# Attention and mixture of experts on one core: a half slot for a half block, gathers one slot later, a reordered last pair

## The chip, the cores and the metric

The kernel runs on one core of a Trainium2 chip. The metric is the time of one execution on the device in microseconds (us); three executions were timed. TensorE (PE) multiplies, ScalarE (ACT) and VectorE (DVE) evict and split, GpSimd (POOL) issues the indirect transfers, SyncE (SP) issues the other loads and stores.

## The reference

```python
# attention: 8 batches, 8 heads, 576 positions, 64 wide, with rotary embedding of q and k
scores = matmul(rotate(q), rotate(k).T) / 8
x = softmax(scores) @ v              # as 4608 tokens x 512
# mixture of experts, one expert per token, 8 experts, hidden width 1024
logits = x @ w_gate + modality_bias[modality_id]
e_idx = argmax(logits); gate_w = softmax(logits)[e_idx]
for e in range(8):
    mask = e_idx == e
    out[mask] = gate_w[mask] * (relu(x[mask] @ w1[e]) @ w2[e])
```

With the inputs that are timed, three experts get tokens: expert 1 gets 1143, expert 6 gets 2289, expert 7 gets 1176. In blocks of 256 rows these are 5, 9 and 5, with 119, 241 and 152 rows in the last blocks.

## The kernel before, in words

Attention comes first: 32 pairs of heads (four pairs a batch), one after the other, with the work of neighbouring pairs interleaved. The order of TensorE, ScalarE, VectorE and POOL is written out by hand: each piece of work has a key, a place in time within its pair (`KEYS`, with overrides for the first, second and last pair in `AT`), one pair is `PER` = 14.438 long, and the jobs are issued in the order of their keys. Program order is queue order on each of these engines. For a pair there are nine score products (S), row minima (MN) and exponentials (EX), six groups of transposes of the probabilities (fills F0 to F3, FA, FB) with evictions by ScalarE (A_) and VectorE (B_), two products with V (AVA for the first 256 columns, AVB for the rest), their evictions (OT), the output products (OUT) and evictions (EV).

Routing runs beside it. For each batch, `route` finds the expert and the place of each token; `scatter` writes token number and gate weight into a table in DRAM (TAB), five indirect transfers a batch. `plan0` makes the plan (PLA) of the first NA = 8 blocks from the first five batches; `plan` makes the plan (PLB) of the rest from all, in VectorE operations on one row; the last batch's routing, its scatters and `plan` lie in a list (`late`) of which `one()` issues one item at fixed places of the expert slots.

The experts run in slots of 256 rows. Slot s takes row numbers and gate weights from TAB (`m_ix`), gathers its rows from X into XG[s % 2] in eight indirect transfers on POOL (`m_gather`, with index arithmetic before the first), transposes them on VectorE (`m_tr`) and splits them into a high part (ScalarE) and a low part (VectorE) (`m_tre`). Weights are loaded by SP into ST1 and ST2 only where the expert changes, and split again in each slot (`m_split`, high part on ScalarE, low part on VectorE). L1 (`m_l1`, line 799) is four groups of 24 matmuls, three for each product (high x high, high x low, low x high); `m_l1e` evicts a group. L2 (`m_l2`, line 816) is two halves of 24 matmuls of 512 columns, one for each 128 rows; each is scaled by the gate weight on ScalarE (line 819) and written to its tokens' rows by an indirect transfer on POOL (line 820).

Slots 0 to 18 (8 of the first plan, NB_STATIC = 11 of the second) always run; a conditional tail (`tc.If`) runs the rest where the plan has more. In `chain`, a slot s issues in this order: gathers for slot s + 2, indices of s + 3, weight loads, then four times (split of W2, group of L1, eviction, one late item), transposes and splits of the rows of slot s + 1, L2 of its first half, two splits of W1, L2 of its second half, two splits of W1. The gathers of the first three slots, and the work of slot 0, have keys in `AT` (`rows`, `l1`, `l1e` and so on): the gathers of slot 1 after the first L1 group of slot 0, those of slot 2 at key 16.5, between the second and the third of the five table scatters of the seventh batch.

Of the kernel before, what the change touches and what calls it, by code (L numbers as in the profile page):

```python
# [18 lines left out]
P = 128  # L19
# [3 lines left out]
BLK = 256  # L23
NA = 8
NB_MAX = 17
NB_STATIC = 11

# [56 lines left out]
def tile_attention_moe(ctx: ExitStack, tc: tile.TileContext, qk, v, mod, wg, mb, w1, w2, rope, cf, ci, out):  # L84
# [18 lines left out]
    PLA = cst.tile([1, 3, NB_MAX], I32, name="PLA")  # L103
    PLB = cst.tile([1, 3, NB_MAX], I32, name="PLB")
    TOT = cst.tile([1, 1], I32, name="TOT")
# [506 lines left out]
    def plan():  # L612
# [18 lines left out]
        tri = cview("TRI")[0:1].rearrange("p (a b) -> p a b", b=E)  # L631
        t88 = t1("t88", [E, E])
        V_.tensor_tensor(t88, tri, nb.unsqueeze(1).to_broadcast([1, E, E]), op=ALU.mult)
        yield
# [18 lines left out]
        V_.tensor_tensor(ch, es[:, 1:ns + 1], es[:, 0:ns], op=ALU.subtract)  # L653
        V_.tensor_scalar(pl[:, 2, 0:ns], ch, 0.0, None, op0=ALU.not_equal)
        yield

# [43 lines left out]

    slots = [(0, i) for i in range(NA)] + [(1, i) for i in range(NB_MAX)]
    ms = {}
# [9 lines left out]
    def m_ix(s):  # L712
        d = ms[s]
        ix = d["ix"] = ixp.tile([P, 2, 2], I32, name="ix", tag="ix")
        i1 = nc.sync.dma_start(out=ix, in_=TAB[bass.ds(d["r"], BLK), :].rearrange("(p t) w -> p t w", t=2)).ins
# [12 lines left out]
    def m_gather(s, t, g, after=None):  # L728
        d = ms[s]
        if "iy" not in d:  # L730
            d["iy"] = ixp.tile([P, 8], I32, name="iy", tag="iy")
            nc.gpsimd.tensor_scalar(d["iy"], d["xi"][:, :, 0], 4.0, cview("I4"), op0=ALU.mult, op1=ALU.add)
        rows = (N if slots[s][0] else NPL * S) * 4
        inst = nc.gpsimd.indirect_dma_start(out=XG[s % 2][:, t, g, :], out_offset=None,  # L734
                                            in_=X.rearrange("n (i f) -> (n i) f", f=P)[0:rows],
                                            in_offset=bass.IndirectOffsetOnAxis(ap=d["iy"][:, 2 * g + t:2 * g + t + 1], axis=0),
                                            bounds_check=rows - 1, oob_is_err=False)
# [5 lines left out]
    def m_rows(s):  # L743
        for t in range(2):
            for g in range(4):
                m_gather(s, t, g)

# [55 lines left out]
    def m_l1e(s, g):  # L803
        d = ms[s]
        ps = d["ps", g]
        sl = slice(g * 2, g * 2 + 2)
        nc.scalar.activation(d["hh"][:, sl, :], ps, AF.Relu)
        nc.vector.scalar_tensor_tensor(d["hl"][:, sl, :], ps, 0.0, d["hh"][:, sl, :].bitcast(F32), op0=ALU.max, op1=ALU.subtract)

    def m_l2(s, t):  # L810
        d = ms[s]
        ps = bank("Y")
        m = 0
        for c in range(8):
            for hx, w in ((d["hh"], W2[0]), (d["hl"], W2[0]), (d["hh"], W2[1])):
                nc.tensor.matmul(ps, hx[:, c, t * P:(t + 1) * P], w[:, c, :], start=(m == 0), stop=(m == 23))  # L816
                m += 1
        y = yp.tile([P, DM], F32, name="y", tag="y")
        nc.scalar.activation(y, ps, AF.Copy, scale=d["ix"][:, t, 1:2].bitcast(F32))  # L819
        nc.gpsimd.indirect_dma_start(out=out, out_offset=bass.IndirectOffsetOnAxis(ap=d["ix"][:, t, 0:1], axis=0),  # L820
                                     in_=y, in_offset=None, bounds_check=N - 1, oob_is_err=False)
# [35 lines left out]

    OV = {0: AT["first"], 1: AT["second"], z: AT["last"]}
    for n in range(NPAIR):
# [34 lines left out]
        if n % 4 == 3:  # L894
# [26 lines left out]
    assert min(A["w2"]) > max(K["T1"], K["LO"]) and min(A["te"]) > max(K[f"S{u}"] for u in range(9)) - PER  # L921
    assert min(A["hi2"]) > fills + 0.05 and min(A["lo2"]) > A["last"]["AVB"] + 0.05 and min(A["l1"]) > fills
# [35 lines left out]
    def prefetch(s):  # L958
# [4 lines left out]
        for i in range(3):  # L963
            m_ix(s + i)
        for i in range(2):
            m_rows(s + i)
        for g in range(4):
            m_load2(s, g)

    def chain(lo, hi, begun):  # L970
# [6 lines left out]
        for s in range(lo, hi):  # L977
            nxt = s + 1 < hi
            if nxt:
                if s + 2 < hi and (not begun or s > 0):  # L980
                    m_rows(s + 2)
                if s + 3 < hi and (not begun or s > 0):
# [6 lines left out]
            if not begun or s > lo:  # L989
                for g in range(4):  # L990
                    m_split(1, g)
                    m_l1(s, g)
                    m_l1e(s, g)
                    one()
            if nxt:
                for t in range(2):
                    m_tr(s + 1, t)
                for t in range(2):
                    m_tre(s + 1, t)
                    one()  # L1000
# [4 lines left out]
            if nxt:  # L1005
# [3 lines left out]
                one()  # L1009
            m_l2(s, 1)  # L1010
            if nxt:
# [4 lines left out]

    ns = NA + NB_STATIC
    chain(0, ns, True)
    order.close()
    tot = nc.values_load(TOT[0:1, 0:1], min_val=0, max_val=NB_MAX)  # L1020
    with tc.If(tot > NB_STATIC):
        prefetch(ns)
        chain(ns, NA + NB_MAX, False)

# [99 lines left out]
```

## Time and profile before

| what | us |
|---|---|
| median of 3 runs | 939.65 (937.27 to 940.5) |
| the profiled execution, its own time | 946.46 |
| its span, first to last instruction | 944.7 |
| TensorE busy in the span | 903.4 |
| attention in the span, to the first matmul of L1 | 497.5 |

The profile is of one execution, and that one took 6.8 us more than the median of the timed ones. Lines of the profile name an engine, a line of the kernel, the operation, what it writes and reads, and how long it took. Matmuls are pipelined: one that is shown with 0.28 or 0.39 us may start 0.117 or 0.233 us after the one before it. A number in brackets is the idle time of that engine before the instruction and what ended it.

### The profile page before, as it was taken

Reading aid. Unit: us, or ns where it says so; the run is one execution under the profiler, and the core shown is the slowest. Engines: PE = TensorE matmul, PEld = TensorE weight load, DVE = VectorE, ACT = ScalarE, POOL = GpSimd, SP = SyncE. Lnnn points to the kernel's source line nnn. Section 1 sums busy time; section 2 is a strip of 40 time slices with the busy share of each in tenths; the row PEclk is TensorE's granted clock in tenths of the full one; section 3 lists DMA queues with packets and bytes.
Section 4 is the critical chain, followed back from the end, with each engine's and each line's share of the span. In section 5 each row is a group of like instructions: output and inputs, shape, how many; then the busy total and the mean of one; then the engine's idle time right before and its main releaser. Section 6 shows DMA issues by size and latency. Waiting matters only on the chain. (4 is left out here: it accounts for less than half of the span.)

```text
span 944.7 us, 24944 instructions
## 1 busy us (share of the span) xinstructions
PE 903.4 (96%) x9248; PEld 740.9 (78%) x9248; DVE 670.6 (71%) x1165; ACT 629.9 (67%) x1292; POOL 669.0 (71%) x498
## 2 busy tenths in 40 slices
PE   2999999999999999999989999999999999999996
PEld 2777777777777777777667878888888899999995
DVE  6677778787787877877784768676666766666661
ACT  2778778787787877878881555565665656666561
POOL 3988879888888898999723768766676656666400
PEclk9999999999999999999999999999999999999998
DMA  8865758768586686855922621117711611251100
GB/s 261 237 185 166 236 159 213 188 167 229 162 222 165 183 213 175 232 163 154 244 98 73 186 72 35 46 57 229 230 51 51 229 40 45 90 190 45 37 24 16
DMA packets 79292, 136.90 MB, mean 145 GB/s; under 512 B 28699, under 2 KB 50603, under 8 KB 78140
## 3 DMA queue, kind: packets, MB, share of 16 engines
q1 hardware_dynamic: 68460, 114.06, 42.8%
q0 software_dynamic: 9440, 19.46, 6.3%
q10 hardware_dynamic: 1264, 1.72, 0.6%
q8 instruction: 75, 1.23, 0.6%
q14 instruction: 53, 0.43, 0.2%
HBM read 140.59 MB, written 19.77 MB: 170 GB/s over the span
## 5 line engine op out<-in xcount | busy, mean ns | idle before, releaser
L328 ACT ACTIVATE P<-ps,mn 128x576 f32<-128x576 f32 x288 | 210.4, 737 | 92.4 <-DVE mn L321 91.9
L321 DVE TENSOR_REDUCE mn<-ps 128x1 f32<-128x576 f32 x288 | 204.1, 745 | 93.5 <-PE ps L312 55.6
L734 POOL DMA_INDIRECT XG<-X,iy x152 | 187.7, 1235 | 70.9 <-issue 53.5
L799 PE MATMUL psH<-HL,W1H 128*128 128x256 f32 x1152 | 205.5, 281 | 1.0 <-issue 0.7
L312 PE MATMUL ps<-SW 64*128 64x288 f32 x960 | 166.5, 314 | 16.0 <-DMA SW<-HL 16.0
L799 PEld LDWEIGHTS psH<-HL,W1H 128*128 128x128 f32 x1152 | 177.9, 188 | 4.1 <-issue 2.5
L312 PE MATMUL ps<-HL 64*128 64x288 f32 x960 | 166.4, 312 | 1.0 <-ACT P L328 0.8
L799 PE MATMUL psH<-HL,W1L 128*128 128x256 f32 x576 | 161.7, 281 | 1.4 <-issue 0.8
L312 PEld LDWEIGHTS ps<-SW 64*128 64x128 f32 x960 | 134.2, 189 | 27.4 <-DMA SW<-HL 15.5
L312 PEld LDWEIGHTS ps<-HL 64*128 64x128 f32 x960 | 136.4, 189 | 22.7 <-issue 13.6
L269 DVE TENSOR_TENSOR W1L<-ST,W1H 128x1024 fp32r<-128x1024 f32 x76 | 90.1, 1222 | 80.6 <-ACT W1H L272 77.5
L390 PE MATMUL pa<-PH,V 128*64 128x320 f32 (+1 forms) x1024 | 138.3, 412 | 2.7 <-ACT oT L272 1.4
L820 POOL DMA_INDIRECT out_dram<-y,ix x38 | 42.9, 1128 | 129.7 <-ACT y L819 97.4
L816 PE MATMUL psY<-W2H,SW 128*128 128x512 f32 x304 | 121.2, 399 | 0.0
L816 PE MATMUL psY<-W2L,SW 128*128 128x512 f32 x304 | 119.9, 394 | 0.0
L334 PE MATMUL ps<-idf,P 64*128 64x64 f32 x2624 | 105.3, 229 | 8.5 <-ACT P L328 2.8
L334 PEld LDWEIGHTS ps<-idf,P 64*128 64x128 f32 x2624 | 92.2, 140 | 23.8 <-ACT PH L272 9.5
L799 PEld LDWEIGHTS psH<-HL,W1L 128*128 128x128 f32 x576 | 108.4, 188 | 1.8 <-issue 1.0
L289 POOL TENSOR_TENSOR HL<-ST,HL 128x1216 fp32r<-128x1216 f32 x31 | 86.1, 2777 | 31.8 <-ACT HL L272 31.7
L390 PEld LDWEIGHTS pa<-PH,V 128*64 128x64 f32 x1024 | 68.1, 136 | 51.1 <-issue 10.1
L366 DVE COPY PH<-ps 128x512 f32<-128x512 f32 (+1 forms) x160 | 96.0, 633 | 8.9 <-PE ps L334 7.6
L269 DVE TENSOR_TENSOR W2L<-ST,W2H 128x1024 fp32r<-128x1024 f32 x76 | 92.6, 1219 | 5.2 <-ACT W2H L272 4.3
(173 smaller groups left out, 1589.9 us busy)
## 6 DMA issues: line engine op xcount, KB each, us to landing
ST<-in_moe_w_dram SPq DMA_DIRECT2D x152, 512.0 KB
ST<-in_qk_dram SPq DMA_DIRECT2D x62, 608.0 KB
SW<-HL SPq DMA_DIRECT2D x124, 232.0 KB
V<-in_v_dram SPq DMA_DIRECT2D x32, 256.0 KB
X<-X SPq DMA_DIRECT2D x8, 1024.0 KB
XG<-X,iy POOLq DMA_INDIRECT x152
V<-in_v_dram SPq DMA_DIRECT2D x64, 16.0 KB
X<-XT SPq DMA_DIRECT2D x16, 64.0 KB
```

Of the source, the lines that this page charges most:

```text
L269: nc.vector.tensor_tensor(o, a, b, op=ALU.subtract)
L289: e.tensor_tensor(d["HL"][:, 1, c], a, d["HL"][:, 0, c].bitcast(F32), op=ALU.subtract)
L312: free(nc.tensor.matmul(ps[:, g, 0:288], t[:, wq, q0:q0 + P], t[:, wk, k0:k0 + 288], start=(m == 0), stop=(m == len(L) - 1)), seen)
L321: lastmin[d["ring", u]] = nc.vector.tensor_reduce(mn, d["S", u][:, :, 0:288], op=ALU.min, axis=AX.XY).ins
L328: nc.scalar.activation(p.rearrange("p (a b) -> p a b", a=2), ps[:, :, 0:288], AF.Exp, bias=d.pop(("m", u)), scale=-1.0, accum_out=d["sum"] ...
L334: free(nc.tensor.transpose(ps[0][:, g, c:c + 64], src[r, k0:k0 + P], idf[r, r]), ps[1])
L366: mine.append((nc.vector.tensor_copy if g else acopy)(o, i).ins)
L390: i = nc.tensor.matmul(pa[hh * 64:hh * 64 + 64, 0:c1 - c0], d["V"][:, hh, kt, :], r, start=(kt == 0), stop=(kt == 4))
L734: inst = nc.gpsimd.indirect_dma_start(out=XG[s % 2][:, t, g, :], out_offset=None, in_=X.rearrange("n (i f) -> (n i) f", f=P)[0:rows], in_o ...
L799: l1_[s] = nc.tensor.matmul(ps[:, i, :], w[:, c, f0:f0 + P], x[:, c, :], start=(m == 0), stop=(m == 11)).ins
L816: nc.tensor.matmul(ps, hx[:, c, t * P:(t + 1) * P], w[:, c, :], start=(m == 0), stop=(m == 23))
L820: nc.gpsimd.indirect_dma_start(out=out, out_offset=bass.IndirectOffsetOnAxis(ap=d["ix"][:, t, 0:1], axis=0), in_=y, in_offset=None, bounds ...
```

## The change

One block of one expert that is at most half full gets a slot of 128 rows. `plan` counts, for each expert, whether its last block holds at most 128 rows, takes the first such expert, takes one block off it, and writes a plan entry for the half slot (24 operations more on VectorE). NB_STATIC becomes 10, and the half slot comes behind the ten as the last one that always runs. In it, half as many rows are gathered, transposed, split and evicted, and there is one half of L2 instead of two; it is computed in two parts of 256 columns, the first evicted by ScalarE, the second by VectorE and ScalarE in halves. L1 runs on all 256 columns as before.

The gathers of slot s + 1 are issued in slot s, a pair before each L1 group; from the second pair on they wait for the group of L1 before. In slot 0 (gathers of slot 1) the pairs wait for the groups that their keys put before them. The gathers of slot 2, which had keys, are issued in slot 1.

In the last pair of attention F2 and FB go before FA, AVB before AVA, and the eviction EVA of the pair before it goes ahead of AVB.

```diff
-NB_STATIC = 11
+NB_STATIC = 10
-           (7, 4.75, (30, "out", 1))), ((0, 11.15, ("l1", 0)),), ((0, 16.5, None),)),
+           (7, 4.75, (30, "out", 1))), ((0, 11.15, ("l1", 0)), (2, 11.33, ("l1", 0)), (4, 11.365, ("l1", 0)), (6, 11.43, ("l1", 0)))),
-    last=dict(AVA=10.3, AVB=10.4, RE=10.2, RI=10.25, OTA=10.96, OTB=11.0, OUTB=11.2, OUTA=11.21, EVB=11.35, EVA=11.4, XO=11.9),
+    last=dict(F2=7.0, A_F2=7.75, B_F2=7.75, FB=7.5, A_FB=8.3, B_FB=8.3, FA=8.35, A_FA=8.8, B_FA=8.8, AVB=10.3, AVA=10.4, RE=10.2,
+              RI=10.25, OTB=10.96, OTA=11.0, OUTB=11.2, OUTA=11.21, EVB=11.35, EVA=11.4, XO=11.9),
+    last2=dict(EVA=24.55),
 # plan():
+        V_.tensor_scalar(ni, nf, float(BLK // 2 - 1), None, op0=ALU.add)
+        nc.vector.tensor_scalar(ni, ni, 8, None, op0=ALU.logical_shift_right)
+        hm = t1("hm", [E])
+        V_.tensor_copy(hm, ni)
+        V_.tensor_tensor(hm, hm, AB, op=ALU.subtract)
+        V_.tensor_tensor(hm, nb, hm, op=ALU.subtract)
...
+        V_.tensor_tensor(nb, nb, hm, op=ALU.subtract)
...
+        V_.memset(pl[:, 2, NB_STATIC:NB_STATIC + 1], 1)
-    slots = [(0, i) for i in range(NA)] + [(1, i) for i in range(NB_MAX)]
+    slots = [(0, i) for i in range(NA)] + [(1, i) for i in range(NB_STATIC)] + [(2, NB_MAX)] + [(1, i) for i in range(NB_STATIC, NB_MAX)]
+    halves = lambda s: range(1 if slots[s][0] == 2 else 2)
 # m_l1e(s, g):
+        n = P * len(halves(s))
+        hh, hl = (d[x][:, g * 2:g * 2 + 2, 0:n] for x in ("hh", "hl"))
 # m_l2(s, t):
+        cut = (0, DM // 2, DM) if slots[s][0] == 2 else (0, DM)
+        for a, b in zip(cut, cut[1:]):
+            ps = bank("Y")[:, 0:b - a]
...
+                    nc.tensor.matmul(ps, hx[:, c, t * P:(t + 1) * P], w[:, c, a:b], start=(m == 0), stop=(m == 23))
...
+            if a:
+                h = (a + b) // 2
+                nc.vector.tensor_scalar(y[:, h:b], ps[:, h - a:], gate, None, op0=ALU.mult)
+                b = h
+            nc.scalar.activation(y[:, a:b], ps[:, 0:b - a], AF.Copy, scale=gate)
 # jobs:
-                late = steps + scats + [(each, next) + ((g, None),) * 4] * 7
+                late = steps + scats + [(each, next) + ((g, None),) * 4] * 13
-    for s in range(3):
+    for s in range(2):
         for i in range(8):
 # chain():
-                if s + 2 < hi and (not begun or s > 0):
-                    m_rows(s + 2)
                 for g in range(4):
                     m_split(1, g)
+                    if nxt:
+                        for i in (2 * g, 2 * g + 1)[:4 * len(halves(s + 1)) - 2 * g]:
+                            m_gather(s + 1, i // 4, i % 4, ("l1", s) if g else None)
                     m_l1(s, g)
                     m_l1e(s, g)
                     one()
-            m_l2(s, 1)
+            if len(halves(s)) > 1:
+                m_l2(s, 1)
-    ns = NA + NB_STATIC
+    ns = NA + NB_STATIC + 1
```

## Rows read from the trace of the kernel before

**Rows 1.** Busy time of each engine in windows that are one L1 or one L2 long: L1 of slots 1 and 2, L1 and L2 of a steady slot (slot 13). The first column is start, end and length in us; PEclk is the granted clock.

```profile
526.23:538.80 12.57, 11.92 (x103) 11.66 (x102) 11.54 (x21) 8.29 (x11) 10.42 (x8) 1.00 0.87 199
550.10:565.31 15.21, 13.45 (x98) 12.03 (x98) 10.11 (x12) 8.84 (x11) 9.30 (x7) 1.00 0.15 49
...
801.47:812.73 11.26, 11.26 (x97) 11.26 (x96) 8.69 (x9) 8.06 (x10) 8.57 (x6) 1.00 0.12 41
812.73:823.92 11.19, 11.19 (x50) 9.03 (x49) 6.54 (x8) 5.24 (x6) 5.35 (x5) 1.00 0.30 88
```

**Rows 2.** Timeline of TensorE at the end of attention: the two products with V of the last pair, and the first matmuls of L1 of slot 0. Columns: start in us, length in us, engine, line, operation, out<-in, count, idle time before and its releaser.

```profile
490.81 1.95 PE L390 MATMUL pa<-PH,V 128*64 128x256 f32 x16 [1.28 <-ACT re L406]
...
494.62 2.38 PE L390 MATMUL pa<-PH,V 128*64 128x320 f32 x16 [1.43 <-ACT oT L272]
...
497.46 0.51 PE L799 MATMUL ps<-HL,W1H 128*128 128x256 f32 x2
```

**Rows 3.** Timeline of POOL in the steady slot 13 (L1 starts at 801.47): output scatter of the second half of slot 12, index arithmetic, the first and the last of the eight gathers, output scatter of the first half of slot 13.

```profile
802.68 0.99 POOL L820 DMA_INDIRECT out_dram<-y,ix  x1 [4.58 <-ACT y L819]
803.75 2.05 POOL L732 TENSOR_SCALAR iy<-xi,CF 128x8 int32<-128x8 int32 x1
806.08 1.76 POOL L734 DMA_INDIRECT XG<-X,iy  x1 [0.27 <-POOL iy L732]
...
816.73 1.35 POOL L734 DMA_INDIRECT XG<-X,iy  x1 [0.30 <-issue]
819.54 1.01 POOL L820 DMA_INDIRECT out_dram<-y,ix  x1 [1.46 <-ACT y L819]
```

**Rows 4.** Timeline of ScalarE: a copy of 128x128 out of PSUM in the last pair, and the last eviction of the kernel.

```profile
487.90 0.30 ACT L272 ACTIVATE PD<-ps 128x128 f32<-128x128 f32 x1
...
936.44 0.69 ACT L819 ACTIVATE y<-psY,ix 128x512 f32<-128x512 f32 x1 [4.92 <-PE psY L816]
```

**Rows 5.** Timeline of VectorE at the end of attention: transposes of the rows of slot 0, their low parts (HL), a weight split, and the eviction EVA of the pair before the last.

```profile
490.62 1.30 DVE L779 STREAM_TRANSPOSE XG<-XG 128x512 f32<-128x512 f32 x2
...
492.55 2.11 DVE L269 TENSOR_TENSOR HL<-XG,HL 128x512 fp32r<-128x512 f32 x2 [0.53 <-ACT HL L272]
494.57 2.35 DVE L269 TENSOR_TENSOR W1L<-ST,W1H 128x1024 fp32r<-128x1024 f32 x2
496.84 0.41 DVE L437 TENSOR_TENSOR X<-pa,ri 128x256 f32<-128x256 f32 x1
```

**Rows 6.** Windows of one microsecond behind the last gather of the steady slot; the last two columns are the busy share of the DMA engines and GB/s.

```profile
818.00:819.00 1.00, 1.00 (x6) 0.80 (x5) 0.20 (x1) 0.43 (x1) 0.08 (x1) 1.00 0.21 66
819.00:820.00 1.00, 1.00 (x6) 0.79 (x5) 0.00 (x0) 1.00 (x2) 0.46 (x1) 1.00 0.02 4
```

**Rows 7.** Timeline of VectorE in the steady slot: transposes, two low parts of W1.

```profile
814.17 1.30 DVE L779 STREAM_TRANSPOSE XG<-XG 128x512 f32<-128x512 f32 x2
...
820.25 2.36 DVE L269 TENSOR_TENSOR W1L<-ST,W1H 128x1024 fp32r<-128x1024 f32 x2 [2.05 <-ACT W1H L272]
```

**Rows 8.** Timeline of ScalarE in the steady slot: high parts of the rows, eviction of the first half of L2, two high parts of W1.

```profile
814.96 2.06 ACT L272 ACTIVATE HL<-XG 128x512 fp32r<-128x512 f32 x2 [1.43 <-DVE HL L808]
818.57 0.69 ACT L819 ACTIVATE y<-psY,ix 128x512 f32<-128x512 f32 x1 [1.56 <-issue]
819.16 2.00 ACT L272 ACTIVATE W1H<-ST 128x1024 fp32r<-128x1024 f32 x2
```

**Rows 9.** Timeline of POOL in slots 1 and 2, at the edges of the stretches that are counted: indices for slot 2 and, behind them, the last of its eight gathers, three table scatters and the second output scatter of slot 0 (13 instructions, 528.15 to 546.72); the second output scatter of slot 1, then from the first of two table scatters over indices and eight gathers to the last of three more table scatters (14 instructions, 567.78 to 590.03).

```profile
528.15 0.92 POOL L732 TENSOR_SCALAR iy<-xi,CF 128x8 int32<-128x8 int32 x1
...
540.60 1.00 POOL L734 DMA_INDIRECT XG<-X,iy  x1 [0.30 <-issue]
...
545.74 0.98 POOL L820 DMA_INDIRECT out_dram<-y,ix  x1 [0.30 <-issue]
...
565.80 1.68 POOL L820 DMA_INDIRECT out_dram<-y,ix  x1 [4.57 <-issue]
567.78 0.97 POOL L537 DMA_INDIRECT TAB<-VAL,oi  x1 [0.30 <-DVE ni L624]
...
589.11 0.92 POOL L537 DMA_INDIRECT TAB<-VAL,oi  x1 [0.31 <-issue]
```

**Rows 10.** Timeline of VectorE and TensorE at the end of slot 1: the second transpose of the rows of slot 2, and the third matmul of L1 of slot 2.

```profile
546.73 0.71 DVE L779 STREAM_TRANSPOSE XG<-XG 128x512 f32<-128x512 f32 x1 [3.80 <-DMA XG<-X,iy]
...
551.37 0.39 PE L799 MATMUL psH<-HL,W1L 128*128 128x256 f32 x1 [0.76 <-issue]
```

**Rows 11.** Timeline of VectorE at the end of slot 2: the two low parts of the rows of slot 3, with plan operations behind each, and the first weight split of W1.

```profile
569.82 1.10 DVE L269 TENSOR_TENSOR HL<-XG,HL 128x512 fp32r<-128x512 f32 x1 [0.64 <-issue]
...
571.98 1.09 DVE L269 TENSOR_TENSOR HL<-XG,HL 128x512 fp32r<-128x512 f32 x1
...
573.64 1.22 DVE L269 TENSOR_TENSOR W1L<-ST,W1H 128x1024 fp32r<-128x1024 f32 x1
```

**Rows 12.** Windows with the granted clock (the column behind the five engines) in L1 of slot 0 and around the two gaps at the end of attention.

```profile
508.00:512.00 4.00, 2.19 (x15) 1.66 (x14) 1.77 (x2) 0.00 (x0) 3.33 (x3) 1.00 0.18 52
512.00:516.00 4.00, 3.67 (x16) 3.14 (x15) 0.45 (x1) 0.60 (x1) 0.00 (x0) 0.57 0.06 16
...
490.00:497.00 7.00, 4.76 (x38) 2.96 (x40) 6.47 (x10) 4.54 (x7) 0.00 (x0) 1.00 0.01 2
```

More of the change, by code (lines that the diff above doesn't have):

```diff
@@ L103, in tile_attention_moe @@
     PLA = cst.tile([1, 3, NB_MAX], I32, name="PLA")
-    PLB = cst.tile([1, 3, NB_MAX], I32, name="PLB")
+    PLB = cst.tile([1, 3, NB_MAX + 1], I32, name="PLB")
     TOT = cst.tile([1, 1], I32, name="TOT")
@@ L632, in plan @@
         t88 = t1("t88", [E, E])
+        V_.tensor_scalar(ni, nf, float(BLK // 2 - 1), None, op0=ALU.add)
+        yield
+        nc.vector.tensor_scalar(ni, ni, 8, None, op0=ALU.logical_shift_right)
+        yield
+        hm = t1("hm", [E])
+        V_.tensor_copy(hm, ni)
+        yield
+        V_.tensor_tensor(hm, hm, AB, op=ALU.subtract)
+        yield
+        V_.tensor_tensor(hm, nb, hm, op=ALU.subtract)
+        yield
+        V_.tensor_tensor(t88, tri, hm.unsqueeze(1).to_broadcast([1, E, E]), op=ALU.mult)
+        yield
+        hc = t1("hc", [E])
+        nc.vector.tensor_reduce(hc, t88, op=ALU.add, axis=AX.X)
+        yield
+        V_.tensor_scalar(hc, hc, 1.0, None, op0=ALU.is_equal)
+        yield
+        V_.tensor_tensor(hm, hm, hc, op=ALU.mult)
+        yield
+        V_.tensor_tensor(nb, nb, hm, op=ALU.subtract)
+        yield
+        V_.tensor_tensor(hc, nb, AB, op=ALU.add)
+        yield
+        V_.tensor_scalar(hc, hc, float(BLK), float(-E * N), op0=ALU.mult, op1=ALU.add)
+        yield
+        V_.tensor_tensor(hc, hc, EBv, op=ALU.add)
+        yield
+        V_.tensor_tensor(hc, hc, hm, op=ALU.mult)
+        yield
+        hr = t1("hr", [1])
+        nc.vector.tensor_reduce(hr, hc, op=ALU.add, axis=AX.X)
+        yield
+        V_.tensor_scalar(hr, hr, float(E * N), None, op0=ALU.add)
+        yield
+        V_.tensor_copy(pl[:, 1, ns:ns + 1], hr)
+        yield
+        V_.tensor_tensor(hc, hm, cview("W8")[0:1], op=ALU.mult)
+        yield
+        nc.vector.tensor_reduce(hr, hc, op=ALU.add, axis=AX.X)
+        yield
+        V_.tensor_scalar(hr, hr, -1.0, float(E), op0=ALU.mult, op1=ALU.add)
+        yield
+        V_.tensor_scalar(hr, hr, float(E - 1), None, op0=ALU.min)
+        yield
+        V_.tensor_copy(pl[:, 0, ns:ns + 1], hr)
+        yield
+        V_.memset(pl[:, 2, ns:ns + 1], 1)
+        yield
         V_.tensor_tensor(t88, tri, nb.unsqueeze(1).to_broadcast([1, E, E]), op=ALU.mult)
@@ L654, in plan @@
         V_.tensor_scalar(pl[:, 2, 0:ns], ch, 0.0, None, op0=ALU.not_equal)
+        yield
+        V_.memset(pl[:, 2, NB_STATIC:NB_STATIC + 1], 1)
         yield
@@ L714, in m_ix @@
         ix = d["ix"] = ixp.tile([P, 2, 2], I32, name="ix", tag="ix")
+        if slots[s][0] == 2:
+            nc.sync.dma_start(out=ix[:, 0, :], in_=TAB[bass.ds(d["r"], P), :])
+            xi = d["xi"] = ixp.tile([P, 8, 2], I32, name="xi", tag="xi")
+            nc.sync.dma_start(out=xi[:, 0:4, :], in_=TAB[bass.ds(d["r"], P), :].rearrange("(q g) w -> q (g w)", g=4).unsqueeze(0).to_broadcast([4, 32, 8]))
+            return
         i1 = nc.sync.dma_start(out=ix, in_=TAB[bass.ds(d["r"], BLK), :].rearrange("(p t) w -> p t w", t=2)).ins
@@ L741, in m_gather @@
                               mybir.DependencyInfo(mybir.DependencyClass.Sync, mybir.DependencyReason.DATA), reason="place")
[L743 to L746, printed above, removed]
     def m_load1(s, g):
@@ L856, in tile_attention_moe @@
     z = NPAIR - 1
-    OV = {0: AT["first"], 1: AT["second"], z: AT["last"]}
+    OV = {0: AT["first"], 1: AT["second"], z - 1: AT["last2"], z: AT["last"]}
     for n in range(NPAIR):
@@ L921, in tile_attention_moe @@
     assert min(A["w2"]) > max(K["T1"], K["LO"]) and min(A["te"]) > max(K[f"S{u}"] for u in range(9)) - PER
-    assert min(A["hi2"]) > fills + 0.05 and min(A["lo2"]) > A["last"]["AVB"] + 0.05 and min(A["l1"]) > fills
+    assert min(A["hi2"]) > fills + 0.05 and min(A["lo2"]) > A["last"]["AVA"] + 0.05 and min(A["l1"]) > fills
     for s in range(len(A["plan"])):
@@ L964, in prefetch @@
             m_ix(s + i)
-        for i in range(2):
-            m_rows(s + i)
+        for i in range(8):
+            m_gather(s, i // 4, i % 4)
         for g in range(4):
@@ L995, in chain @@
             if nxt:
-                for t in range(2):
+                for t in halves(s + 1):
                     m_tr(s + 1, t)
-                for t in range(2):
+                for t in halves(s + 1):
                     m_tre(s + 1, t)
@@ L1022, in tile_attention_moe @@
         prefetch(ns)
-        chain(ns, NA + NB_MAX, False)
+        chain(ns, len(slots), False)
 CF_OFF = {}
```

23 lines of the change are left out of this document (11 added, 12 removed).

## The prediction

> **What bounds the kernel now.** I read the busy windows first, stage by stage, because a share over the whole span mixes the attention with the experts. In a steady slot the first product (L1, 96 matmuls of 256 columns) takes 11.26 us and the second (L2, 48 matmuls of 512 columns) 11.19 us, and TensorE is busy for all of both [rows 1]: 0.117 and 0.233 us a matmul, 22.45 us a slot. From slot 3 to the last matmul the time is the sum of TensorE's work; whatever comes later than TensorE wants it is paid in full, and whatever is taken from TensorE is won in full. TensorE is not full before that: at the end of attention it stands 1.28 us before the first product with V and 1.43 us before the second [rows 2], and L1 of slots 1 and 2 takes 12.57 and 15.21 us where 11.26 would do [rows 1].
>
> Next I read the queue of GpSimd (POOL), because the change moves its gathers. In a steady slot that starts at 801.47 it issues the scatter of the previous slot's second half at 802.68, the index arithmetic at 803.75 and eight gathers from 806.08 to 818.08 [rows 3]. These gathers are for the slot after next, so they have a whole slot of slack. That is why POOL can be far behind in the first slots at little cost to TensorE.
>
> **Taken away: half of L2 in the last slot.** The inputs need five, nine and five blocks of 256 rows, 19 in all, and one expert's fifth has 119 rows. The new plan finds it, so 18 full blocks and one half remain and the conditional tail stays shut. L1 of the half still runs on 256 columns: nothing won there. L2 is one half in two column parts: 48 matmuls of 256 columns, 48 x 0.117 = 5.63 us in place of 11.19 [rows 1], **-5.6 us** on the path that sets the end. The last eviction took 0.69 us on ScalarE for 128x512; now two engines share 128x256, and a ScalarE copy of 128x128 took 0.30 [rows 4]: **-0.4 us**. The half comes last, so its expert's weights are loaded once more, in slot 17. Such loads held gathers back by some 4 us in slot 1 (below); here only four gathers are issued and end some 5 us earlier than eight would, which covers it. Uncovered it would cost up to 4.
>
> **Moved: the last pair.** The product that needs no F1 goes first and can start once F2 and FB are out; evicting the earlier pair's output before it frees the second accumulator. Both waits [rows 2] can go, 2.7 us. But L1 of slot 0 also needs the low part of its rows, which VectorE ends at about 494.6, and the eviction that moves ahead of the transposes (0.41 us and a shorter second instruction, 0.6 together [rows 5]) pushes that to 495.3. So L1 starts at about 495.4 and not 497.46 [rows 2]: **-2.1 us** (0 to -2.7).
>
> **Moved: the gathers, slots 0 and the steady ones.** In slot 0 the last pair of gathers now waits for the end of L1. Queued behind it is the first output scatter, which needs half of L2, 5.6 us; two gathers take 2.6. No cost. In later slots the gathers stand in the same place of POOL's queue, but the next slot waits for them. The pacing waits do not bind: L1's groups end 2.8, 5.6 and 8.4 us into the slot, and POOL comes to its third, fifth and seventh gather later than that [rows 3]. The chain: last gather issued 818.08 [rows 3]; DMA is still busy in the next microsecond and idle in the one after [rows 6], so landed near 819.3; transpose 0.65 [rows 7], high part 1.03, the eviction queued behind it 0.6, first weight split 1.0 [rows 8], low part of the weights 1.2 [rows 7]: 823.8. TensorE wants it for its third matmul at 823.92 + 0.23 = 824.15. It fits by 0.3 us: **0**; if it misses by 0.3 us, 13 slots make 4 us, the upper bound.
>
> **Moved: the gathers, slots 1 to 3.** Here POOL also carries ten scatters into the routing table, and now nothing may be late. (Times are those of the profile of before, the 2.1 us left out.)
>
> Slot 1. From 528.15 to 546.72 POOL does 13 instructions: indices, eight gathers, three table scatters, one output scatter [rows 9]. The change keeps the 13 and puts the indices and gathers last, so the last gather is issued at 546.7 instead of 541.60. In before its transpose waited for the landing until 546.73, 5.1 us after the issue, beside the weight loads [rows 10]. By 546.7 those are over, so I take the steady 1.2 us: 547.9, and the third matmul of slot 2 moves from 551.37 [rows 10] to 552.6: **+1.3 us** (0 if the landing is no later; 4 if the four scatters put ahead cost 2.06 us each, like the first gather of a steady slot [rows 3], and not 1.3 [rows 9]).
>
> Slot 2. POOL's order becomes: second output scatter of slot 1, two table scatters, indices, eight gathers with three table scatters among them. In before the same 14 behind that output scatter stand from 567.78 to 590.03, 22.25 us [rows 9]. The output scatter needs an eviction that ScalarE does behind the late rows: 547.9 and 0.65 (transpose), 1.03, 0.6, two weight splits of 1.0, 0.69 and a hand-over of 0.3 give 553.1, and 1.0 for the scatter 554.1. Then the last gather is issued at 576.4, landed at 577.6, transposed at 578.3. VectorE's stretch from the first subtraction to the start of the weight split took 3.82 us with two groups of plan operations in it [rows 11]; with 1.2 for the split, 583.3. TensorE could go at 552.6 + 22.45 = 575.1. **A stall of +8.2 us.** Lower bound: every POOL step at 1.3 us [rows 9], 18.2 and not 22.25: 4. Upper bound: 1.75 a step, between the gathers of a steady slot [rows 3]: 10.4.
>
> Slot 3. No table scatters, but the plan's 24 new small VectorE operations (13 groups of four instead of 7) reach into it, two groups between the subtractions: 3.82 less two subtractions of 1.05, 1.7 us [rows 11]. POOL starts this slot early, after the stall, and covers part: **+1 us** (0 to 2.7). Groups that fall elsewhere lie in VectorE's idle time.
>
> **The clock.** From 508 to 512 us TensorE was busy 2.19 of 4 us at granted clock 1.00, and from 512 to 516 it got 0.57, most of it at the 1.2 GHz level; after that it was at 2.4 GHz again. Around gaps of 1.3 and 1.4 us the clock stayed 1.00 [rows 12]. A stall of 8 us is worse than the first case: 4 x 0.43 = **+1.7 us**, once (0 to 3.4).
>
> The Trainium skill, "TensorE: Matmul & The Clock Gate", section "Why this matters for your kernels", asks that matmul bursts have no long idle gaps between them, or the clock falls back. It speaks against this change: by that rule a long stall costs more than its length. The trace agrees [rows 12], and my sum has it; without the rule's effect the sum would be +2.4.
>
> What a POOL step costs decides the sum. The indices took 2.05 us and a first gather 1.76 [rows 3], a gather at 540.60 only 1.00 [rows 9]. I take the longer sums, because in slots 1 to 3 the steps fall beside VectorE's weight splits.
>
> The Trainium skill, "GPSIMD Engine Reference", section "1. Specifications", says that GpSimd shares its SBUF interfaces with VectorE and contends with VectorE's two-input instructions, as the splits are. By the price without contention the sum would be -1.8 us, by that with it +4.1. The spread of the rows agrees with the rule [rows 3, 9].
>
> **Sum.** -5.6 - 0.4 - 2.1 + 1.3 + 8.2 + 1.0 + 1.7 = +4.1 us. Against the profiled execution (span 944.7, time 946.46) it is less: its L1 of slot 2 lost 15.21 - 11.26 = 3.95 us [rows 1], 1.0 of it to the late weight split, and the other 2.9 would now pass inside the stall of slot 2: +1.2, 947.7. That execution was 6.8 us above the median of the runs, 939.65. The losses in slots 0 to 2 that no named wait explains are the likely difference, so I count them as absent there and add 4 us to the median: **943.6 us**, 0.4% slower.
>
> **Rivals.** *A, POOL keeps up: faster.* Place: the last gather for slot 3. If POOL does the 14 steps of slot 2 in 16 us and not 22, the stalls of slots 1 to 3 come to about 2 us in all and the clock holds: -8.1 + 2 = -6.1, 933.5. It decides at a sum of stalls of 5 us. For it: single steps of 1.0 and 0.3 us between [rows 9]. Against: both sets of before took more than that [rows 9].
> *B, stall and gain cancel:* 1.3, the lower bound of 4, and 1.0, no fall of the clock: -8.1 + 6.3 = -1.8, 938.
> *C, every slot is late:* the 0.3 us of slack is a lack of 0.5 in 13 slots, 6.5 us on top of my sum: 950.
> *D, the half is not found:* the conditional tail runs seven more slots, 7 x 22.45 = 157 us and more. The row counts speak against it.
>
> **How the numbers follow.** Chances: my case 0.50, A 0.28, B 0.13, C 0.08, D 0.01. A measurement of this kernel tells 0.3%, 2.8 us, from no change. Slower: 0.42 of mine, C and D, 0.51. Same: 0.08 of mine, 0.02 of A, 0.10 of B, 0.20. Faster: the rest of A and B, 0.29. My case alone: 938 (slot 2 at its lower bound) to 951 (upper bounds of slots 1 and 2, and of the clock). Over all, 934 to 951 leaves out about half of A's lower side and the upper end of C, 0.2.
>
> **What would show it.** Right: L2 of the last slot at 5.6 us; L1 of slot 0 some 2 us earlier; TensorE idle 7 to 10 us before the third matmul of slot 3, the wait ended by VectorE's weight split behind a transpose that waited for a gather; no gap in later slots. Wrong: no such gap (POOL's 14 steps shorter, or the order of its queue another), a gap in every slot, or L1 of slot 0 held by something else.

## The result

The changed kernel took 945.96 us (median of 5 runs, 943.97 to 948.09) against 939.22 for the kernel before (5 runs, 936.93 to 940.5): a ratio of 1.008, 95% interval 1.0062 to 1.0098, so slower by 5.8 to 9.2 us. 943.6 was forecast. The profiled execution took 948.09 us, its span is 946.3.

The page of the changed kernel: its span, TensorE's busy time, and the granted clock in 40 slices.

```profile
span 946.3 us, 24973 instructions
PE 897.0 (95%) x9248; PEld 738.1 (78%) x9248; DVE 676.1 (71%) x1188; ACT 625.5 (66%) x1291; POOL 651.4 (69%) x493
PEclk9999999999999999999999998999999999999998
```

Windows of the changed kernel, columns as in [rows 1]: a part of L1 of slot 0; L1 of slot 2; L2 of slot 2 with the gap behind it; L1 of slot 3; a whole steady slot (4); slot 7; L2 of the half slot.

```profile
508.00:512.00 4.00, 4.00 (x26) 3.56 (x25) 1.62 (x2) 1.20 (x2) 3.09 (x4) 1.00 0.19 53
546.98:560.95 13.97, 13.22 (x97) 13.01 (x98) 11.52 (x13) 8.95 (x11) 9.54 (x9) 0.88 0.19 48
560.95:576.11 15.16, 11.26 (x51) 8.82 (x49) 5.57 (x16) 4.27 (x6) 8.79 (x9) 0.99 0.21 27
576.11:591.19 15.08, 14.10 (x97) 13.80 (x97) 14.43 (x44) 8.93 (x11) 10.05 (x10) 0.78 0.18 62
602.30:624.70 22.40, 22.40 (x145) 20.32 (x144) 14.20 (x16) 13.24 (x16) 13.87 (x11) 1.00 0.12 37
669.61:693.78 24.17, 22.94 (x145) 20.30 (x145) 15.61 (x17) 13.13 (x17) 13.08 (x12) 1.00 0.64 218
931.27:937.13 5.86, 5.86 (x50) 5.65 (x48) 0.43 (x1) 0.86 (x2) 0.00 (x0) 1.00 0.01 3
```

The half slot is there: its L2 takes 5.86 us, and 11.36 in the last slot of the kernel before:

```profile
925.00:936.36 11.36, 11.36 (x50) 8.84 (x48) 0.88 (x2) 1.28 (x2) 0.97 (x1) 1.00 0.05 16
```

Slot 4 is full of TensorE's work. L1 of slots 2 and 3 takes 13.97 and 15.08 us where 11.31 would do, at granted clocks of 0.88 and 0.78, and there is a gap ahead of slot 3. The timeline of TensorE names the gaps: the two products with V of the last pair and the start of L1 of slot 0, then the first and third matmuls of L1 of slots 2 and 3, and the third of slots 17 and 18.

```profile
491.16 2.38 PE L392 MATMUL pa<-PH,V 128*64 128x320 f32 x16
...
493.90 1.90 PE L392 MATMUL pa<-PH,V 128*64 128x256 f32 x16
496.16 0.80 PE L857 MATMUL ps<-HL,W1H 128*128 128x256 f32 x2
...
546.98 0.51 PE L857 MATMUL psH<-HL,W1H 128*128 128x256 f32 x2 [2.71 <-ACT W1H L274]
548.24 0.38 PE L857 MATMUL psH<-HL,W1L 128*128 128x256 f32 x1 [0.75 <-DVE W1L L271]
...
576.11 0.80 PE L857 MATMUL psH<-HL,W1H 128*128 128x256 f32 x2 [3.90 <-ACT W1H L274]
577.88 0.58 PE L857 MATMUL psH<-HL,W1L 128*128 128x256 f32 x1 [0.98 <-DVE W1L L271]
...
898.00 0.38 PE L857 MATMUL psH<-HL,W1L 128*128 128x256 f32 x1 [0.76 <-DVE W1L L271]
...
920.21 0.28 PE L857 MATMUL psH<-HL,W1L 128*128 128x256 f32 x1
```

The two waits of [rows 2] are gone from the last pair. In exchange TensorE stands 3.5 us ahead of slot 2's third matmul and 4.9 us ahead of slot 3's, for both halves of a weight split. VectorE's and ScalarE's timelines show what holds the splits: second transposes of the rows of slots 2, 3, 7 and 13; for slot 3 also the low parts of the rows, one of the plan's operations (L647) and the first weight split, and on ScalarE the eviction and the high parts queued behind the rows. ScalarE's last row is the last eviction of the kernel.

```profile
543.63 0.71 DVE L837 STREAM_TRANSPOSE XG<-XG 128x512 f32<-128x512 f32 x1 [1.72 <-DMA XG<-X,iy]
...
572.76 0.71 DVE L837 STREAM_TRANSPOSE XG<-XG 128x512 f32<-128x512 f32 x1 [5.75 <-DMA XG<-X,iy]
573.39 1.03 DVE L271 TENSOR_TENSOR HL<-XG,HL 128x512 fp32r<-128x512 f32 x1
...
574.88 1.07 DVE L271 TENSOR_TENSOR HL<-XG,HL 128x512 fp32r<-128x512 f32 x1
...
576.24 0.21 DVE L647 TENSOR_TENSOR t<-CF,hm 1x64 f32<-1x64 f32 x1
...
576.62 1.20 DVE L271 TENSOR_TENSOR W1L<-ST,W1H 128x1024 fp32r<-128x1024 f32 x1
...
666.24 0.71 DVE L837 STREAM_TRANSPOSE XG<-XG 128x512 f32<-128x512 f32 x1 [2.68 <-DMA XG<-X,iy]
...
802.18 0.71 DVE L837 STREAM_TRANSPOSE XG<-XG 128x512 f32<-128x512 f32 x1 [4.47 <-DMA XG<-X,iy]
```

```profile
574.46 0.65 ACT L886 ACTIVATE y<-psY,ix 128x512 f32<-128x512 f32 x1
575.00 2.00 ACT L274 ACTIVATE W1H<-ST 128x1024 fp32r<-128x1024 f32 x2
...
937.55 0.37 ACT L886 ACTIVATE y<-psY,ix 128x128 f32<-128x128 f32 x1 [2.71 <-DVE y L884]
```

POOL's timeline: in slot 1 the last gather for slot 2; in slot 2 the second output scatter of slot 1, the first of two table scatters, the indices and the last gather for slot 3 (14 steps from 551.82 to 571.15); the last gathers for slots 7 and 13.

```profile
539.57 1.00 POOL L797 DMA_INDIRECT XG<-X,iy  x1 [0.30 <-issue]
...
550.11 1.40 POOL L887 DMA_INDIRECT out_dram<-y,ix  x1 [2.55 <-ACT W1H L274]
551.82 1.96 POOL L539 DMA_INDIRECT TAB<-VAL,oi  x1 [0.30 <-DVE W1L L271]
...
555.14 0.47 POOL L794 TENSOR_SCALAR iy<-xi,CF 128x8 int32<-128x8 int32 x1
...
570.15 1.00 POOL L797 DMA_INDIRECT XG<-X,iy  x1 [0.30 <-issue]
...
662.37 1.00 POOL L797 DMA_INDIRECT XG<-X,iy  x1 [0.31 <-issue]
...
799.52 1.00 POOL L797 DMA_INDIRECT XG<-X,iy  x1 [0.30 <-issue]
```

Read slot 3 backwards. The third matmul waits for W1L (576.62 to 577.82), that for W1H (575.00), that for an eviction (574.46) behind the high part of rows whose transpose began at 572.76, when the gather issued until 571.15 had landed. L2 of slot 2 was done at 572.2. From the end of the last issue to the third matmul are 6.7 us. Two pieces of them are other work of the engines in between: 0.65 of the eviction on ScalarE, and some 0.6 of plan operations on VectorE, which stand between the end of the second low part (575.95) and the weight split (576.62) when the high part is ready at 576.05. The chain starts at the end of POOL's queue.

### The profile page after: what moved, and what is told of

It reads as the page before. It is cut to its first block, busy times and chain, and to the rows that moved or that the text cites. A ratio compares the mean times of both kernels' runs of the same rounds, so it can differ in the third digit from the quotient of the medians.

```text
span 946.3 us, 24973 instructions
## 1 busy us (share of the span) xinstructions
PE 897.0 (95%) x9248; PEld 738.1 (78%) x9248; DVE 676.1 (71%) x1188; ACT 625.5 (66%) x1291; POOL 651.4 (69%) x493
## 5 line engine op out<-in xcount | busy, mean ns | idle before, releaser
L857 PE MATMUL psH<-HL,W1H 128*128 128x256 f32 x1152 | 207.7, 283 | 7.2 <-ACT W1H L274 7.1
L797 POOL DMA_INDIRECT XG<-X,iy x148 | 164.7, 1113 | 69.0 <-issue 50.1
L887 POOL DMA_INDIRECT out_dram<-y,ix x37 | 50.7, 1369 | 147.1 <-ACT y L886 108.7
L880 PE MATMUL psY<-W2H,SW 128*128 128x512 f32 (+1 forms) x304 | 118.0, 388 | 0.0
L880 PE MATMUL psY<-W2L,SW 128*128 128x512 f32 (+1 forms) x304 | 116.7, 384 | 0.0
L274 ACT ACTIVATE HL<-XG 128x512 fp32r<-128x512 f32 x37 | 41.4, 1124 | 104.2 <-DVE XG L837 104.1
L271 DVE TENSOR_TENSOR W1L<-ST,W1H 128x1024 fp32r<-128x1024 f32 x76 | 90.3, 1224 | 17.8 <-ACT W1H L274 17.5
```

What stands on the lines that cost most here:

```text
L271: nc.vector.tensor_tensor(o, a, b, op=ALU.subtract)
L857: l1_[s] = nc.tensor.matmul(ps[:, i, :], w[:, c, f0:f0 + P], x[:, c, :], start=(m == 0), stop=(m == 11)).ins
L880: nc.tensor.matmul(ps, hx[:, c, t * P:(t + 1) * P], w[:, c, a:b], start=(m == 0), stop=(m == 23))
```

## The experiments

They ran four at a time on three chips, where the kernel before took 938.0, 947.8 and 948.4 us; so between batches only ratios and stretches of traces are compared. The stretches are the times from the start of L1 of slot 1 to that of slot 4 (3 x 22.41 = 67.2 if TensorE never waits), from slot 4 to 6 (44.8) and from 6 to 18 (268.9). They come from one profiled execution each, which can lie off the median of its runs: 4.1 us below in pair_only, 6.6 below in all_late, where it is the fastest of twelve, 3.5 above in half_only, 5.5 above in changed_again.

```
                       ratio to before (95%)      1-4    4-6    6-18
before, first profile  1                         72.72  44.91  269.88
changed                1.0080 (1.0062, 1.0098)   81.65  44.81  272.86
move_only              1.0158 (1.0132, 1.0184)   82.83  44.91  272.15
pair_only              0.9982 (0.9965, 0.9998)   68.79  44.91  269.44
half_only              0.9924 (0.9900, 0.9947)   72.13  44.81  268.88
half_pair              0.9904 (0.9881, 0.9926)   68.54  44.81  268.88
scat_late              0.9934 (0.9899, 0.9969)   73.46  45.82  275.73
all_late               0.9978 (0.9945, 1.0010)   68.25  48.98  274.49
no_pace                1.0075 (1.0036, 1.0113)   85.82  44.52  276.25
half_pair_all_late     0.9894 (0.9841, 0.9946)   71.53  44.81  271.01
changed_again          1.0041 (1.0008, 1.0074)   81.44  50.88  279.53
all_late_again         0.9957 (0.9920, 0.9995)   69.59  54.94  274.73
all_late_iy            0.9913 (0.9878, 0.9948)   69.12  50.36  269.66
half_pair_again        0.9888 (0.9848, 0.9927)   80.74  44.81  268.88
```

**Each part alone.** move_only is the kernel before with the gathers moved (the edit, shortened):

```diff
-    m_rows(s + 2)                  # at the start of slot s
+    m_gather(s + 1, i // 4, i % 4, ("l1", s) if g else None)   # a pair ahead of each group of L1 of slot s
```

> The kernel before with the gathers moved and nothing else. Theory (the moved gathers carry the whole loss: the stalls of 3.5 us in slot 2 and 4.9 us in slot 3 of the changed kernel, and two falls of the clock there): it loses what the changed kernel lost (6.7 us) and what the other two parts won on top (8 to 9.5 us), so 952 to 956 us against 939, with both gaps in its trace. Rival (the stalls come with the new plan's 24 VectorE operations, or with the earlier start of slot 0): the moved gathers alone cost under 3 us, 939 to 942, and no gap over 2 us in slot 3.

953.58 us against 938.0; by the ratio +14.8 (12.4 to 17.3). The theory held: the loss lies in the moved gathers, without the half, its plan or the new last pair. Its trace has the same waits, here all of TensorE's between 515 and 605 us:

```profile
PE psH L794 <- ACT W1H L272: 8.0, 2, 6.4
PE psH L794 <- DVE W1L L269: 2.7, 3, 1.2
```

pair_only has the new keys of the last two pairs alone (`last=dict(F2=7.0, ...)`, `last2=dict(EVA=24.55)`).

> The kernel before with the last pair reordered and nothing else. Theory: L1 of slot 0 starts 2 to 3.5 us earlier and the slots behind it all move up by as much: 935.5 to 937 us against 939. Rival (what is won in front of slot 0 is given back in slots 0 to 2, where gathers and table scatters come no earlier): within 1 us of the kernel before.

936.3 against 938.0, -1.7 (-3.3 to -0.2), which lies between the theory and its rival and decides for neither. In the traces the first product with V of the pair before the last and the start of L1 of slot 0 lie 17.98 us apart in the kernels with the new pair (pair_only, half_pair and the changed kernel's first profile) and some 20.86 in half_only and move_only: 2.9 us. The traces from the other two chips have 18.4 to 18.7 with the new pair, and none with the old one to set beside them. Of the 2.9 some 0.3 goes again at once: the second matmul of L1 waits for the low part of the rows, so that the first two take 0.80 us (496.16 above) and not 0.51 as in half_only.

half_only has the half slot, its plan and its L2, with `m_rows(s + 2)` and the old pair.

> The kernel before with the half slot and its plan, gathers and last pair as before. Theory: L2 of the last slot 5.6 us and the last eviction 0.4 us shorter, and nothing else moves: 933 us against 939. Rival (the extra load of weights in slot 17 or the longer plan costs something where gathers are early too): over 935.

932.59 against 938.0; by the ratio -7.1 us (-9.4 to -5.0). L2 of its last slot takes 5.85 us. A full slot that waits for nothing takes 22.41 us in the kernels with the half slot and 22.45 in those without, some 0.7 us over 17 slots; no run shows why.

half_pair is the changed kernel with `m_rows(s + 2)` back in its place.

> The changed kernel with its gathers put back where they stood. Theory: both gains and no stall of slot 3: 929.5 to 931.5 us against 939, and 946 for the changed kernel. Rival (the stalls of the changed kernel come from its earlier slot 0 or its longer plan): over 937, with a gap over 2 us before the third matmul of slot 3.

929.32 us, by the ratio -9.0 (-11.2 to -6.9), the fastest of the batch. Its three stretches, from slot 1, 4 and 6:

```profile
517.48:586.02 68.54, 67.75 (x440) 61.21 (x439) 56.50 (x115) 40.00 (x50) 50.26 (x43) 1.00 0.37 105
586.02:630.83 44.81, 44.81 (x290) 40.62 (x288) 30.67 (x32) 26.81 (x32) 33.01 (x26) 1.00 0.19 60
630.83:899.71 268.88, 268.88 (x1730) 243.71 (x1728) 181.32 (x190) 158.74 (x191) 152.69 (x124) 1.00 0.37 123
```

From slot 4 to 18 TensorE is never idle, with all 24 new plan operations and the extra weight load in slot 17. The parts add up: -1.7 - 7.1 + 14.8 = +6.0, and half_pair with the move on top +5.8; the changed kernel has +7.5 by its ratio.

**Is it the length of POOL's queue?** scat_late leaves the changed kernel's gathers alone and moves the last batch's five table scatters out of slot 2, behind the gathers of slot 3:

```diff
-late = steps + scats + [(each, next) + ((g, None),) * 4] * 13
+late = steps + [(each, next) + ((g, None),) * 4] * 13 + [(each, None)] * 3 + scats
```

> The changed kernel with the last batch's five table scatters put behind POOL's gathers of slot 3 (the plan's operations come five places earlier in VectorE's queue for it). Theory (the stall of slot 3 is the length of POOL's queue in slot 2): the last gather of slot 2 is issued five steps of 1.3 us earlier, the wait of 4.9 us before the third matmul of slot 3 falls to under 1 us and the second fall of the clock (3.3 us) goes with it: 7 to 8 us less than the changed kernel, 938 to 939. The wait in slot 2 stays. Rival (the stall comes from the plan's operations on VectorE or from how late gathers land): less than 2 us won.

The edit also brings the plan's operations five places forward; move_only, which has the stall without the 24 new ones, and half_pair, which has them without the stall, speak against these as its cause. The wait of slot 3 is gone, that of slot 2 stays, and the first stretch is 8.2 us shorter than the changed kernel's. All waits of TensorE from 515 to 605 us (in all, times, longest):

```profile
PE psH L857 <- ACT W1H L274: 2.3, 1, 2.3
PE psH L857 <- DVE W1L L271: 1.5, 2, 0.8
```

all_late does the same with the batch before it, which stood at the turn of slots 0 and 1.

> As the one with the last batch's table scatters late, and the five of the batch before it put behind the gathers of slot 3 too, the last batch's behind those of slot 4. Theory: in slot 1 too the gathers are issued some 8 us earlier, the wait of 3.5 us in slot 2 and the first fall of the clock (1.7 us) go as well: 933 to 935 us; what is left over the kernel with the old gathers (929) are the slots 7, 8, 14 and 17 and the chain in them. Rival (in slot 2 the landing beside the weight loads sets the wait, not POOL's queue): no more than 1.5 us under the one with only the last batch late.

Its three stretches:

```profile
520.42:588.67 68.25, 67.54 (x440) 61.00 (x438) 56.14 (x114) 40.05 (x50) 41.24 (x36) 1.00 0.33 109
588.67:637.65 48.98, 46.33 (x289) 40.45 (x288) 30.16 (x33) 26.61 (x32) 31.15 (x29) 1.00 0.15 41
637.65:912.14 274.49, 271.28 (x1729) 244.06 (x1728) 185.12 (x191) 157.06 (x191) 155.34 (x128) 1.00 0.37 122
```

The first stretch is 13.4 us under the changed kernel's, the sum that was expected (4.9 + 3.5 and 5.0 for the clock), and the clock is 1.00 throughout. So the loss in slots 1 to 3 is POOL's queue. Yet the time did not come to 933 to 935, not even by ratio (0.9978 x 939.2 = 937.1): slots 4 and 5 lose 4.2 us where the scatters now stand ahead of the gathers (the last gather's issue ends 17.8 and 18.7 us into the slot), 1.3 of it in waits with no releaser, and slots 6 to 17 lose 5.6. By the ratios all_late is no faster than scat_late.

no_pace drops the gathers' waits for the groups of L1 (`None` in place of `("l1", s) if g else None`).

> The changed kernel without the waits of the gathers for the groups of L1, from slot 1 on. Theory: POOL comes to each pair later than its group of L1 ends, so nothing changes: 945 to 947 us. Rival (the waits hold POOL up in the first slots or in the steady ones): over 3 us faster.

Ratio 1.0075, that of the changed kernel within intervals of 2 and 4 us either way: the pacing waits cost nothing that these can tell. Its first stretch is longer by 4.2 us, but 5.4 us of it are waits with no releaser.

half_pair_all_late is half_pair with all ten scatters late, and with slot 0's gathers paced as in the changed kernel.

> The kernel with the half slot, the reordered last pair and the old gathers, with all ten table scatters of the last two batches put behind the gathers of slots 3 and 4. Theory: the gathers have a slot of slack there, so the scatters delay nothing that TensorE waits for; what can go is the 1.3 us that L1 of slot 1 loses to a late weight split beside those scatters: 928 to 929.3 us against 929.3. Rival (the scatters hold up the early slots there too): 926 or less.

Ratio 0.9894 against 0.9904, no difference that the intervals (5 us either way) can tell. With a slot of slack no cost of the scatters' place shows.

**Why slots 6 to 17 lose.** changed_again and half_pair_again repeat two kernels so that the four can be compared on one chip.

> The changed kernel as it is, once more beside the three below on the same chip. Ratio to the kernel before 1.006 to 1.010 if it is as in its first measurement. By its trace it loses 4 us in slots 4 to 17 against 14 slots of 22.41; the first measurement of the kernels with late scatters showed 8 to 10 us there, on another chip. If that belongs to the chip and not to the scatters, this kernel loses 6 us or more there on such a chip too.

> The kernel with all ten table scatters late, once more. Theory: on the same chip it is 11 to 14 us under the changed kernel, since the waits of slots 2 and 3 and both falls of the clock are gone and the slots behind lose what they lose in the changed kernel. Rival (the scatters in slots 3 and 4 or something they set off cost what was won): less than 8 us under it.

> All ten table scatters late, and the index arithmetic for a slot's gathers done half a slot earlier, ahead of the output scatter of the previous slot's second half. Theory (the chain from the last gather to the third matmul misses by some tenths in the late slots, because POOL comes to the gathers too late): POOL starts the gathers 1 to 2 us earlier, slots 4 to 17 fall to 22.41 each, and the time comes to within 2 us of the kernel with the old gathers. Rival (the landing of the gathers or the weight splits set these losses, not POOL's queue): slots 4 to 17 lose as much as with all ten late alone.

> The half slot and the reordered last pair with the old gathers, once more on the chip of the three others: ratio to the kernel before 0.988 to 0.993, 15 to 18 us under the changed kernel, slots 4 to 17 at 22.41 each.

all_late_iy computes the indices half a slot earlier:

```diff
+            if s + 2 < hi:
+                m_iy(s + 2)        # was: with the first gather of slot s + 1
             if len(halves(s)) > 1:
                 m_l2(s, 1)
```

On this chip: changed 953.09, all_late 944.72, all_late_iy 939.84, half_pair 938.28 (before 948.41). The changed kernel's ratio is 1.0041 where 1.006 to 1.010 was expected; the intervals of its two measurements overlap. Its trace loses 16.7 us in slots 4 to 17, more than the 6 that were to tell a loss of the chip from one of the scatters, but most of it in three slots with waits that no named cause explains (4, 8 and 14: 28.47, 24.43 and 26.68 us), so this stays open. all_late is 8.4 us under the changed kernel and not 11 to 14. In the traces it wins 11.9 in slots 1 to 3; slots 4 and 5 are 4.1 longer, but each of the two traces has one slot there with such a wait (28.47 and 29.78 us), so this is no price of the scatters. all_late_iy wins 5 more by its median, and 5 in slots 6 to 17, where it was expected; in slots 4 and 5 it still loses 5.5, with such a wait in slot 5 too. First all_late_again from slot 6 to 18, then all_late_iy:

```profile
645.02:919.75 274.73, 271.15 (x1729) 243.74 (x1728) 184.06 (x190) 157.16 (x191) 156.82 (x128) 1.00 0.36 120
```

```profile
638.66:908.32 269.66, 269.63 (x1730) 244.00 (x1728) 184.32 (x191) 157.93 (x191) 170.15 (x128) 1.00 0.37 124
```

5.8 us of loss became 0.8. Slot by slot, from third matmul to third matmul, five other traces with moved gathers and the half agree (changed twice, scat_late, all_late twice; slots 6 to 16, 55 in all). Where the last gather's issue ends by 16.55 us into the slot (20), the median is 22.43; where it ends later, up to 18.35 (35), it is 23.02. no_pace adds 7 and 4 and leaves the second as it is and the first at 22.41. The means hardly differ (22.9 and 23.0), because the first group holds some of the long slots with unnamed waits. In slot 12 of the changed kernel it ends at 800.52 - 784.22 = 16.3. With the indices early it ends by 16.55 in every slot from 6 to 16. The landing adds its part: in slot 6 of the changed kernel the issue ends at 663.36 and the transpose starts at 666.24, 2.9 us later, and in slot 12 1.7 us (800.52 to 802.18); slot 7, where weights are loaded (DMA share 0.64, and 0.12 in slot 4), has 3.4 and takes 24.17. In slots 9 and 13, with weight loads too (0.69 and 0.70), it is 1.6 and 1.9.

So the moved gathers, freed of most of the delays found, come to within their interval of the old ones and not ahead of them. The version that beats both kernels is half_pair: 0.9904 and 0.9888 of the kernel before, and 938.28 / 953.09 = 0.984 of the changed one on the same chip (14.8 us, where 15 to 18 were expected).

## Why the prediction was right, point by point

The direction, the place and nearly the size were right. One sign was missed: TensorE was to be idle 7 to 10 us before the third matmul of slot 3 and is for 4.9, mainly because L1 of slot 2 had run slower (below). Slots 1 to 3 are counted from third matmul to third matmul, as the prediction did.

```
term                         forecast   measured in the trace
L2 of the half                 -5.6     -5.5   (5.86 for 11.36)
tail                           -0.4      0
last pair                      -2.1     -2.9
slot 1 (to 548.24)             +1.3     +2.4   (27.59 for 25.14)
slot 2 (548.24 to 577.88)      +8.2     +7.2   (29.64 - 22.41)
slot 3, with the clock         +2.7     +2.3   (577.88 to 602.54, less 22.41)
slots 4 to 17                   0       +3.9   (317.67 - 14 x 22.41)
sum                            +4.1     +7.4
```

Against the 22.45 of a full slot in the kernel before, the sum is 0.7 less: 6.7, the difference of the medians.

- **Half of L2:** right. The extra weight load in slot 17 was to be covered by four gathers that end 5 us earlier; they did (issue over at 908.5, 11.8 into the slot), and though they landed only 4.9 us later, slot 18's third matmul waits for nothing (920.21). Slot 17 takes 23.23 us, but its 0.8 is the wait at its own third matmul (898.00), for gathers of slot 16 whose issue ended 17.6 us into that slot; in move_only, without the half and the load, slot 17 takes 23.54.
- **Tail:** the step failed. Two engines share the eviction, but not at once: ScalarE starts its 128x128 at 937.55, when VectorE's 0.35 us are over, released by `y` of VectorE's line (the row above). The last scatter is issued 1.07 us behind the last matmul, and 1.05 in the kernel before.
- **Last pair:** right in mechanism, undersized in the trace, though not by the times (-1.7 in pair_only). The eviction that moves ahead of the transposes pushed the low part of the rows back by 0.3 and not by 0.6 (from half_only to the changed kernel, counted from the product with V of the pair before): VectorE's copies ahead of it came 0.2 earlier.
- **Slot 1:** its last gather is issued 19.9 us into the slot, and 20.5 was forecast (546.7 - 526.23). The term that failed is the landing: 3.1 us and not the steady 1.2. The weight loads were not over at the end of the issue, 540.57: the DMA engines stay busy until 542.
- **Slot 2:** the 14 steps took 19.3 us and not 22.25, so the choice of the longer sum was too pessimistic by 2.9; but the second output scatter came 1.4 us later relative to the slot's third matmul, and the landing took 1.6. That the term comes out within 1 us is in part luck: errors of opposite sign. The upper bound was misread: 1.75 us a step is said to stand in [rows 3], where the eight gathers are 1.5 apart on the mean, so that by them the bound lies below the value taken; 1.4 was measured. Rival A needed 16.
- **Clock:** it fell twice and not once (0.88 and 0.78). In slot 2, where L1 took 12.71 us from the third matmul on and not 11.08, this cost nothing extra, since TensorE only waited less at the end of the slot; so one fall is paid, as forecast, in slot 3's L1: 591.19 - 577.88 = 13.31 us from the third matmul on for 11.08, 2.2. The plan's operations, forecast at 1.0 in that slot, cost nothing there. The Trainium skill, "TensorE: Matmul & The Clock Gate", section "Why this matters for your kernels", asks for no long idle gaps between bursts; the trace agrees, and all_late, without the gaps, has 1.00 throughout.
- **Slots 4 to 17:** the step that failed. A slack of 0.3 us was read off a single slot; the landing of 1.2 us is 1.6 to 1.7 when quiet, and the end of the issue moves from 16.3 to 17.6 us into the slot. In the changed kernel's trace 2.6 of the 3.9 us lie in slots 6 to 8 (landings of 2.9 and 3.4, and an issue that ends at 17.4) and 0.9 in slots 16 and 17 (an issue that ends at 17.6); the other nine lose 0.2 or less each. So it is not rival C, which has every slot late, though it comes to over half of C's 6.5; scat_late on another chip loses 7.8.
- **The profile of before against its median:** the choice to count the unexplained losses of its slots 0 to 2 as absent is borne out. L1 of slot 0 took 17.21 us there and 13.1 to 13.4 in all four kernels of the first batch; in the changed kernel TensorE is busy for all of 508 to 512 (the window above). Taken against the profiled execution, the forecast would have been +1.2 and "same".

## What to carry to other kernels

Work that moves closer to its consumer turns another queue's length into the critical path: count every instruction ahead of it on the issuing engine, and the landing at its loaded price, before calling it free. A slack of some tenths read from one slot is no slack; read the same interval in many slots, quiet and loaded. When a change mixes parts, cost the best part alone: two of three won 9 us here, and the third gave 15 back.

## What the runs showed of the hardware

**TensorE can stand with nothing to wait for that the profile names.** In some executions it starves so in one slot or a few, not always the same ones (0 and 2 here, 4, 8 and 14 in changed_again, 5 in all_late_again). half_pair_again's profiled execution (948.13 us, where its median is 938.28) has such a burst in slot 2: windows, then three rows of its timeline (PEld is the weight load; remote is a releaser that the profile does not name).

```profile
550.00:554.00 4.00, 2.71 (x20) 2.42 (x19) 1.29 (x3) 0.00 (x0) 3.08 (x4) 1.00 0.18 49
554.00:558.00 4.00, 1.63 (x8) 1.19 (x7) 0.00 (x0) 0.00 (x0) 2.85 (x3) 0.85 0.17 49
558.00:562.00 4.00, 3.63 (x17) 3.51 (x17) 1.74 (x2) 3.41 (x4) 1.69 (x2) 0.50 0.28 109
```

```profile
553.48 0.41 PE L862 MATMUL psH<-HL,W1H 128*128 128x256 f32 x2 [1.17 <-issue]
...
554.91 0.30 PEld L862 LDWEIGHTS psH<-HL,W1H 128*128 128x128 f32 x2 [1.11 <-issue]
...
558.59 0.69 ACT L891 ACTIVATE y<-psY,ix 128x512 f32<-128x512 f32 x1 [8.97 <-remote]
```

TensorE does not stand alone: ScalarE does nothing for 8.97 us, nor VectorE, while POOL goes on issuing (2.85 of 4 us in the second window). The clock fell behind it, and the stretch from slot 1 to 4 took 80.74 us; in half_pair's first execution the same instructions took 68.54. The dip in slot 0 of the kernel before [rows 12] looks the same. What withholds the instructions was not tried and stays open. The profiled executions of the changed kernel's first measurement and of the first batch's four kernels show none of it, those on the second and third chip all show some, which may be why the intervals there are wide.

**A gather's price on POOL** is 1.00 us with 0.30 between when quiet and up to 1.9 in the early part of a slot, beside VectorE's splits; the same index arithmetic took 0.47 and 2.05 us. The Trainium skill, "GPSIMD Engine Reference", section "1. Specifications", says that GpSimd contends with VectorE's two-input instructions; these rows agree, though no run isolated it. From slot 4 on in the changed kernel, none of the 41 gathers that overlap no split on VectorE took more than 1.00 us, and the 67 that overlap one took 0.99 to 2.03.
